# Hash attention and four Fourier-mixing networks on one core: all attention first, masks on TensorE throughout, then the networks in a row

## The chip, the cores and the metric

One Trainium2 chip, one of its cores. The metric is the device time of one execution in microseconds, as the median of several runs. Beside it stands one execution taken by the hardware profiler. TensorE (PE in the profile, its weight loads PEld) multiplies matrices, VectorE (DVE) and ScalarE (ACT) work element by element, GpSimd (POOL) does little here besides issuing transfers, and SyncE (SP) issues most transfers. Every engine runs its own instructions in the order in which they were written for it and waits for the others by semaphores.

## The reference

Batch 4, 8 heads, sequence 768, head size 64; the attention's output, seen as 768 x 512 per batch, goes through a network with a Fourier mixing.

```python
q_bucket = sum((q @ proj > 0) * 2**arange(6)); k_bucket likewise
mask     = q_bucket[..., :, None] == k_bucket[..., None, :]
scores   = where(mask, q @ k.T / sqrt(64), -1e9)
attn     = exp(scores - max); attn = attn / (sum(attn) + 1e-9)
x        = (attn @ v) as (batch, 768, 512)
u        = x + real(fft(fft(x, axis=1), axis=2))
un       = (u - mean(u)) / sqrt(var(u) + 1e-6)
out      = u + relu(un @ w_ch1) @ w_ch2      # 512 -> 2048 -> 512
```

All inputs are float32 except for the weights, which arrive as 64-bit numbers and are narrowed on the chip.

## The kernel before, in words

**Attention.** Two heads make a pair; there are 16 pairs (`n`), four in each batch (`b`). The keys of a pair come in six chunks (`c`) of 128. For one chunk, `scores` (L912) multiplies keys by queries for two halves (`g`) of 384 queries, each half into one of two PSUM buffers `sc`; ACT takes the exponential into a buffer `pk` (L925, of which there are two); `values` (L950) multiplies `pk` into `oo`; a tally (L1044) adds `pk` up on DVE into `acc`, from which `key_sums` (L960) makes the denominators and `scale` the quotient, written to `x`. `prepare` turns queries and keys over and finds their hash bits (L815, L841) for the next pair.

The mask is made in two ways. In pairs 0 to 4 (`LITE`) the hash bits, as plus and minus a large number, are multiplied on TensorE into the same PSUM buffer as the scores (L901), so that a wrong bucket gives an exponential of zero. In pairs 5 to 15 two small matmuls (L855, L865) make bucket numbers, and DVE compares them and multiplies `pk` by the result (L939).

**The network** of a batch, `mix`, has `fold` (DVE sums that use symmetries of the transform and write `z`), two rounds of matmuls `cs` (L1165) and `A`, `B` (L1194) with additions into `x` (L1208), transposes of `x` (`across`, L1220), and `mlp7`. The latter multiplies by a scheme with seven products instead of eight, in an inner half (`inner`: four slices `f` of seven products, L1474, into `h`), an outer half (`outer7`: three groups `j` of seven products, L1353), then a second inner and a second outer half. The left operands of the inner products are sums of quarters of w1, the right ones of the outer products sums of quarters of w2 (the seven names B11 to T4). Network 0 forms them itself: `quarters(f)` makes four sums s1 to s4 in the small buffer `tq` (L1267 to L1270) for the next slice and stores them in DRAM, `weights2` fetches w2, narrows it (`narrow`, L642 to L658) and combines it (L1319 to L1322). Networks 1 to 3 read both back through queues. `tq` also holds temporaries of the outer half, and the spectrum `F` shares its memory with `h`.

**Order.** Attention of batch 0 is written out by hand, with w1 fetched and converted beside it (`weights1`, seven raw buffers). From batch 1 on, `attention(b)` and the network of batch b-1 are generators that a loop advances in turns, so many steps of the network for each chunk; a scheduler with priorities sets the final order, and `behind()` keeps an attention group's matmuls together. Network 3 comes last, alone. PSUM's eight banks are two for `sc`, two for `oo`, two for the rest; only before and after attention may the rest use all of these.

Of the kernel before, what the change touches and what calls it, by code (L numbers as in the profile page):

```python
# [20 lines left out]
P = 128  # L21
# [12 lines left out]
WC = 512  # L34
# [15 lines left out]
def _consts():  # L50
# [23 lines left out]
    pw = np.zeros((P, 2, P))  # L74
    for r in range(P):
        h, bit = divmod(r % 32, NBITS)
        if h < 2:
            pw[r, h] = 2.0**bit


# [13 lines left out]
    for par in range(2):  # L94
# [11 lines left out]
        "pw": np.ascontiguousarray(pw, dtype=np.float32),  # L106
# [379 lines left out]
def _main(  # L486
# [17 lines left out]
    ps_sc = ctx.enter_context(  # L504
        tc.tile_pool(name="ps_sc", bufs=2, space=bass.MemoryType.PSUM)
    )
    ps_o = ctx.enter_context(
        tc.tile_pool(name="ps_o", bufs=2, space=bass.MemoryType.PSUM)
    )
    ps_1 = ctx.enter_context(  # L510
        tc.tile_pool(name="ps_1", bufs=2, space=bass.MemoryType.PSUM)
    )
# [4 lines left out]
    roomy = [True]  # L517
    turn = [0]

    def pt(shape, name):  # L520

        turn[0] += 1
        if roomy[0] and turn[0] % 2:
            if turn[0] % 4 == 1:
                return ps_o.tile(shape, F32, tag="o", name=name)
            return ps_sc.tile(shape, F32, tag="sc", name=name)
        return ps_1.tile(shape, F32, tag="ps", name=name)
# [14 lines left out]
    def load(n, names="qkv", second=nc.sync):  # L542
# [6 lines left out]
        for nm in names:  # L549
            src = {"q": q, "k": k, "v": v}[nm]  # L550
            tag, bufs = ("vn", 2) if nm == "v" else ("qkn", 2)
            tl = wt([P, S], F32, tag, f"{nm}n{n}", bufs)
# [39 lines left out]
    LITE = (0, 1, 2, 3, 4)  # L592
# [6 lines left out]
    own = const.tile([P, 2], F32, tag="own", name="own")  # L599
    nc.sync.dma_start(own, cn["own"].ap())  # L600
    load(0, "v")
    pj = const.tile([P, 32], F32, tag="pj", name="pj")
    nc.gpsimd.memset(pj, 0.0)
    for h in range(2):
        nc.sync.dma_start(pj[h * D : (h + 1) * D, h * NBITS : (h + 1) * NBITS], proj)
    pw = const.tile([P, 2, P], BF16, tag="pw", name="pw")
# [7 lines left out]
    NPK = 2  # L614
    pks = []
    for i in range(NPK):
        pk = const.tile([P, 2, 2, HALF + 1], F32, tag=f"pk{i}", name=f"pk{i}")
        nc.gpsimd.memset(pk[:, :, :, HALF : HALF + 1], EPS)
        pks.append(pk)
# [3 lines left out]
    w2 = const.tile([P, NFC, DM], F32, tag="w2", name="w2")  # L623
# [7 lines left out]
    def narrow(dst, raw, col, low=None):  # L631
# [7 lines left out]
        di = dst.bitcast(I32)  # L639

# [10 lines left out]
        if len(di.shape) == 2:  # L651
            nc.vector.tensor_tensor(di, di, low, op=ALU.add)
        else:
            for i in range(di.shape[1]):
                nc.vector.tensor_tensor(di[:, i], di[:, i], low[:, i], op=ALU.add)
# [38 lines left out]
    class Arrival:  # L694
# [19 lines left out]
        def convert(self, i, low=None):  # L714
            if self.wide:
# [6 lines left out]
                narrow(dst, raw, self.col + i, low)  # L722
            self.fetch(i + self.depth)

    def weights1():
# [6 lines left out]
        ft = wt([P, 12, WC], F32, "F", "fraw", 1)  # L732
        raws = [zt[:, i] for i in range(3)] + [
            ft[:, i : i + 2].rearrange("p i w -> p (i w)") for i in range(0, 8, 2)
        ]
        arrival = Arrival(slices, raws, 0, nc.sync)
        for i in range(arrival.depth):
            arrival.fetch(i)
            if i == 2:
                load(1)  # L740
        yield
        half = None
        for i in range(len(slices)):
            arrival.convert(i, ft[:, 8 + i % 4].bitcast(I32))
            yield
            if half:
                centre(half[0], next(half[1]))
                half = None
            if i % NDC == NDC - 1:


                f = i // NDC * WC
                if f < DFF // 2:
                    half = f, average(f)
                    next(half[1])

# [5 lines left out]
    def norm(n, io, tn):  # L762
        junk = wt([P, S], BF16, "junk", f"sq{io}_{n}", 1)
# [5 lines left out]
    def prepare(n):  # L769

        lite = n in LITE
        ts = {}
        for io, nm in enumerate("qk"):
            tn = nat.pop((nm, n))
            tt = wt([P, S], F32, nm + "t", f"{nm}t{n}")
# [27 lines left out]
        if lite:  # L803

            qk = wt([P, 2, S], BF16, "qb", f"qkb{n}")
            qz = qk[:, 0].rearrange("p (g s) -> p g s", g=2)
            bits = {"q": qz[:, 0], "k": qk[:, 1, 0:HALF]}  # L810
            for io, nm in enumerate("qk"):
                ps = pt([P, HALF], f"bits{nm}{n}")
                for j in range(4):
                    h, g = divmod(j, 2)
                    nc.tensor.matmul(  # L815
                        ps[32 * j : 32 * j + 32, :], pjw[:, h * D : h * D + 32],
                        ts[nm][:, g * HALF : (g + 1) * HALF], start=True, stop=True,
                    )
                nc.vector.tensor_scalar(
                    bits[nm], ps, 0.0, off[:, io : io + 1],  # L820
                    op0=ALU.is_gt, op1=ALU.subtract,
                )
                if io == 0:
                    for g in (1, 0):
                        nc.vector.tensor_scalar(
                            qz[:, g], qz[:, 0], own[:, g : g + 1], None, op0=ALU.mult
                        )
                else:
                    for j in range(4):
                        to, at = (slice(32 * i, 32 * i + 32) for i in (j, j ^ 1))  # L830
                        (evac if n == 0 else nc.vector.tensor_copy)(
# [865 lines left out]
```

## Time and profile before

| | us |
|---|---|
| Median of 3 runs (1073.3 to 1076.49) | 1073.97 |
| Span of the profiled execution, first to last instruction | 1070.7 |
| PE busy | 1036.3 (97%) |
| DVE busy | 779.7 (73%) |
| ACT busy | 489.5 (46%) |
| POOL busy | 64.1 (6%) |

The page gives the profiled execution's span and no other time for it; the median stands 3.3 us above the span, which is taken for what lies around it. A row of the timeline has start, length, engine, line, operation, output and inputs with the shape, and the count; in brackets how long the engine was idle and what ended that. Lengths of pipelined instructions overlap, so costs are best read from start to start. A float32 matmul is two records.

### The profile page before, as it was taken

To read this page: it belongs to the slowest core of one execution; us is meant where nothing else is said; L and a number is where in the kernel's file an instruction comes from. 1 tells how busy PE (TensorE), PEld (TensorE's weight loads), DVE (VectorE), ACT (ScalarE), POOL (GpSimd) and SP (SyncE) were. 2 spreads that over 40 slices of the span, in tenths; PEclk is the share of its full clock that TensorE was granted. 3 is DMA by queue.
4 is the path that set the end of the run, shared out by engine and by line. 5 is a ranking of instruction groups with operands and counts; after the bars stand their busy time and mean duration, and the time that the engine had idled before them with its cause. 6 is when DMAs were issued, how large, how long until landed. Compare 5 with 4: busy or idle time off the path is not lost.

```text
span 1070.7 us, 14177 instructions
## 1 busy us (share of the span) xinstructions
PE 1036.3 (97%) x4983; PEld 635.7 (59%) x4983; DVE 779.7 (73%) x1326; ACT 489.5 (46%) x993; POOL 64.1 (6%) x138
## 2 busy tenths in 40 slices
PE   8999899999999999999999999999999999999997
PEld 4333364457644676546665675555675579668576
DVE  4889969996799967877758877767857874644353
ACT  7888564761386323454236315354325512440420
POOL 2000000011000020100000020010000012200000
PEclk9999999999999999999999999999999999999999
DMA  8754551480154462123062242322042205222301
GB/s 192 217 141 86 113 139 41 135 234 1 35 150 158 125 202 37 44 67 80 12 201 74 66 121 90 59 64 60 15 130 81 65 25 172 65 74 92 125 20 43
DMA packets 172769, 103.15 MB, mean 96 GB/s; under 512 B 126481, under 2 KB 159889, under 8 KB 172689
## 3 DMA queue, kind: packets, MB, share of 16 engines
q1 hardware_dynamic: 166672, 88.25, 30.4%
q0 software_dynamic: 4448, 13.50, 4.2%
q8 instruction: 42, 0.69, 0.3%
q10 hardware_dynamic: 1568, 0.39, 0.2%
q14 instruction: 39, 0.31, 0.1%
HBM read 81.14 MB, written 20.97 MB: 95 GB/s over the span
## 4 chain that ended last, share of the span: by engine, by line
PE 76%; DVE 14%; ACT 4%; issue 2%; DMA 2%; SPq 1%; DVEq 0%; ACTq 0%; POOL 0%; POOLq 0%
PE o L1353 25%; PE h_p L1474 23%; PE oo L950 10%; PE sc L912 9%; PE cs L1165 3%; DVE pk L939 2%; PE A L1194 2%; DVE acc L1044 2%; ACT pk L925 2%; PE B L1194 1%; PE sum L960 1%; SPq L576 1%; DVE x L1208 1%; PE bits L841 1%; DMA qn<-in_q_dram 1%
## 5 line engine op out<-in xcount | busy, mean ns | idle before, releaser
L1353 PE MATMUL o<-w,h 128*128 128x256 f32 x1152 | 258.6, 381 | 0.9 <-DVE w L1365 0.5
L1353 PEld LDWEIGHTS o<-w,h 128*128 128x128 f32 x1152 | 216.7, 190 | 41.6 <-issue 6.4
L925 ACT ACTIVATE pk<-sc 128x768 f32<-128x768 f32 x192 | 147.4, 808 | 78.7 <-PE oo L950 35.8
L1474 PE MATMUL h_p<-x,w 128*128 128x384 f32 x448 | 164.5, 494 | 2.4 <-ACT w L1541 1.7
L939 DVE SCALAR_TENSOR_TENSOR pk<-qb,kb,pk 128x768 f32<-128x768 bf16 x132 | 128.7, 1011 | 39.7 <-ACT pk L925 39.6
L912 PE MATMUL sc<-qt,kt 64*128 64x384 f32 x768 | 153.6, 503 | 1.7 <-ACT pk L925 1.4
L950 PE MATMUL oo<-pk,vn 128*64 128x385 f32 (+1 forms) x768 | 146.2, 495 | 1.5 <-DVE pk L939 1.3
L1474 PEld LDWEIGHTS h_p<-x,w 128*128 128x128 f32 x448 | 81.9, 190 | 68.4 <-issue 9.3
L1474 PE MATMUL h_p<-w 128*128 128x384 f32 x288 | 105.9, 489 | 0.0
L1044 DVE TENSOR_TENSOR acc<-acc,pk 128x1536 f32<-128x1536 f32 (+1 forms) x64 | 98.5, 1549 | 5.4 <-ACT pk L925 5.2
L950 PEld LDWEIGHTS oo<-pk,vn 128*64 128x64 f32 x768 | 50.5, 136 | 86.5 <-issue 74.2
L912 PEld LDWEIGHTS sc<-qt,kt 64*128 64x128 f32 x768 | 66.2, 186 | 55.4 <-issue 19.3
L1474 PEld LDWEIGHTS h_p<-w 128*128 128x128 f32 x288 | 53.7, 190 | 38.8 <-issue 1.6
L1365 DVE SCALAR_TENSOR_TENSOR w<-o,rs,w 128x256 f32<-128x256 f32 x56 | 26.6, 479 | 41.6 <-PE o L1353 41.6
L1383 ACT COPY tq<-o 128x256 f32<-128x256 f32 x24 | 8.9, 372 | 104.5 <-PE o L1353 104.5
L1488 ACT ACTIVATE h<-h 128x384 f32<-128x384 f32 x72 | 37.4, 524 | 28.5 <-DVE h L1530 13.7
L1353 PE MATMUL o<-w 128*128 128x256 f32 x176 | 42.2, 383 | 0.3 <-DVE w L1365 0.2
L1103 POOL DMA_DIRECT2D out_dram<-w x30 | 16.4, 548 | 405.3 <-issue 321.4
L1525 DVE TENSOR_TENSOR h<-h 128x384 f32<-128x384 f32 x32 | 17.7, 555 | 28.9 <-ACT h L1524 28.8
L1353 PEld LDWEIGHTS o<-w 128*128 128x128 f32 x176 | 32.9, 190 | 7.6 <-DVE w L1365 1.2
L1399 DVE TENSOR_TENSOR tq<-tq,o 128x256 f32<-128x256 f32 x24 | 10.0, 417 | 36.4 <-PE o L1353 36.4
L1372 ACT COPY tq<-o 128x256 f32<-128x256 f32 x24 | 8.8, 369 | 60.3 <-PE o L1353 60.2
(175 smaller groups left out, 1316.1 us busy)
## 6 DMA issues: line engine op xcount, KB each, us to landing
w<-ad SPq DMA_DIRECT2D x168, 128.0 KB, 2.1
w<-bd SPq DMA_DIRECT2D x42, 512.0 KB, 4.5
zraw<-in_moe_w_ch_dram POOLq DMA_DIRECT2D x16, 512.0 KB, 3.8
bd<-w SPq DMA_DIRECT2D x14, 512.0 KB, 3.6
vn<-in_v_dram SPq DMA_DIRECT2D x32, 192.0 KB, 3.4
qn<-in_q_dram SPq DMA_DIRECT2D x116, 48.0 KB, 2.5
kn<-in_k_dram SPq DMA_DIRECT2D x58, 96.0 KB, 2.9
zraw<-in_moe_w_ch_dram SPq DMA_DIRECT2D x8, 512.0 KB, 7.1
```

The source lines that it names most:

```text
L912: last[0] = nc.tensor.matmul(ps[:, h, 0:HALF], kt[rows, ks], qt[rows, qs], start=kb is not None or early, stop=not early,)
L925: done_by[ET.Activation] = nc.scalar.activation(pk[:, g, :, 0:HALF], ps[:, :, 0:HALF], AF.Exp, scale=SCALE)
L939: done_by[ET.DVE] = nc.vector.scalar_tensor_tensor(w, qb[:, h].rearrange("p (g s) -> p g s", g=2), kb[:, h, c : c + 1], w, op0=ALU.is_equa ...
L950: oo = nc.tensor.matmul(oos[g][h * D : (h + 1) * D, 0:w], nat["v", n][:, (2 * c + h) * D : (2 * c + h + 1) * D], pk[:, g, h, 0:w], start=( ...
L1044: done_by[ET.DVE] = nc.vector.tensor_tensor(acc[:, g], (first if c == 1 else acc)[:, g], new[:, g], op=ALU.add,)
L1165: nc.tensor.matmul(ps[:, pc + 2 * lo : pc + 2 * hi - 1 : 2], z[:, cp, pc, par, t * P : (t + 1) * P], ch[:, cp, pc, lo:hi], start=(cp == 0) ...
L1194: nc.tensor.matmul(ps[:, cols], F[:, par, k, t, j * P : (j + 1) * P], sq[:, t, k, cols], start=(t == 0), stop=(t == 1),)
L1353: nc.tensor.matmul(ps, a[:, r], right7[i][:, r], start=start and r == 0, stop=r == HF // 2 - 1, skip_group_check=not start,)
L1365: nc.vector.scalar_tensor_tensor(t[:, cols], src, r, t[:, cols], op0=ALU.mult, op1=ALU.add)
L1474: nc.tensor.matmul(ps, left[:, k], right[i][:, k], start=start and k == 0, stop=k == 1, skip_group_check=not start,)
L1488: done_by[ET.Activation] = nc.scalar.activation(h, h, AF.Relu)
L1525: done_by[ET.DVE] = nc.vector.tensor_tensor(c22, c21, c22, op=ALU.add)
```

## The change

- `attention` runs over all 16 pairs in one loop, written out by hand: scores of a chunk, then `values` and tally of the chunk before, with the next pair's `prepare`, a step of `weights1` (three a pair from pair 1 on) and, in the last pair, the fold of batch 0. Key and query loads run two pairs ahead.
- The mask is on TensorE in every pair; `LITE`, the bucket numbers, the mask on DVE, `behind` and the key sums in several parts are gone. All five tallies are DVE additions of 1536 columns.
- There are four `pk` buffers. `x` has one buffer for each batch.
- The attention's memory (`att`) and PSUM pools are closed after the last pair; w2, `tq`, `F`/`h` and a pool of eight PSUM banks are opened in it. The four networks run one after the other. The fold of batch b+1 is written into the second outer half of network b.

```diff
-    LITE = (0, 1, 2, 3, 4)
-    NPK = 2
+    NPK = 4
...
+            first = None
+            for c in range(NT):
+                pk = scores(n, c)
+                first = pk if c == 0 else first
+                done = pending.pop(0) if pending else None
+                if c == 1:
+                    next(ends[0][0], None) if ends else None
+                if done:
+                    m, d, dpk, doos, dfirst, dacc = done
+                    values(m, d, dpk, doos)
+                    tally(d, dpk, dfirst, dacc)
+                    if d == NT - 1:
+                        ends.append([scale(m, doos, dacc)])
+                        next(ends[-1][0])
+                if ends and c in (2, 3):
+                    next(ends[0][0], None)
...
+                if c < NT - 1 if n else c:
+                    next(ahead, None)
+                if n and c in (0, 4, 5):
+                    next(other, None)
+                if c > 1:
+                    next(folds, None)
+                pending.append((n, c, pk, oos, first, acc))
...
+    own.close()
+    late = ctx.enter_context(tc.tile_pool(name="late", bufs=1, reuse_waits="tile"))
+    ps_b = ctx.enter_context(
+        tc.tile_pool(name="ps_b", bufs=8, space=PSUM, reuse_waits="tile")
+    )
...
-            yield from outer7(b, half, hall, ut, rs, ss)
+            ahead = fold(b + 1) if half and b < B - 1 else iter(())
+            for _ in outer7(b, half, hall, ut, rs, ss):
+                next(ahead, None)
+                yield
+            for _ in ahead:
+                pass
...
     for b in range(B):
...
-            for i, _ in enumerate(attention(b), 1):
...
-                while done * steps < (MIX - LEFT) * (i - wait):
-                    next(other)
-                    done += 1
...
         other = mix(b)
         if b == 0:
...
-            other = after(NT, other, islice(arrival2, HF + 2))
+            other = after(NT - 2, other, islice(arrival2, HF + 2))
+        for _ in other:
+            pass
```

On TensorE, the end of a pair in batch 2 before (`oo` of a pair among products `o` of network 1's outer half; two heads share the array when their matmuls stand next to each other):

```order
L1353 MATMUL o_1_0_0_4123<-w_124,h_3092 128x256 x4
L950 MATMUL oo_0_3861<-pk_117,vn_3489 64x385
L1353 MATMUL o_1_0_4_4143<-w_124 128x256 x4
L1353 MATMUL o_1_0_6_4151<-w_124,h_3092 128x256 x4
L1353 MATMUL o_1_0_4_4143<-w_124,h_3092 128x256 x4
L1353 MATMUL o_1_0_5_4164<-w_124,h_3092 128x256 x4
L950 MATMUL oo_0_3861<-pk_117,vn_3489 64x385
L950 MATMUL oo_1_3862<-pk_117,vn_3489 64x384 x2
```

and a chunk of a late pair after the change (L834 masks, L844 scores, L860 values, L878 key sums):

```order
L844 MATMUL sc_0_1_2580<-qt_2395,kt_2421 128x384 x2
L834 LDWEIGHTS qkb_2452
L834 MATMUL sc_1_1_2586<-qkb_2452 128x384
L834 LDWEIGHTS qkb_2452
L834 MATMUL sc_1_1_2586<-qkb_2452 128x384
L844 MATMUL sc_1_1_2586<-qt_2395,kt_2421 128x384 x2
L878 MATMUL sum_2592<-acc_2373,ones 32x384 x4
L860 MATMUL oo_0_2548<-pk_119,vn_2368 64x385 x2
L860 MATMUL oo_1_2549<-pk_119,vn_2368 64x384 x2
```

The network's matmuls are gone from between the two heads' matmuls, and masks have come in.

On DVE, the fold of batch 0 before (L1125 to L1143, between preparations of the next pair and, further on, of pair 5; L1044 is the tally):

```order
L1044 TENSOR_TENSOR acc_845<-acc_845,pk_119 128x768 x2
L1125 TENSOR_TENSOR ef_0_0_953<-x_209 128x768
L1130 TENSOR_TENSOR ef_0_0_953<-ef_0_0_953 128x384 x2
L1139 TENSOR_TENSOR z_952<-ef_0_0_953 128x2x95
L1139 TENSOR_TENSOR z_952<-ef_0_0_953 128x2x96
L1139 TENSOR_TENSOR z_952<-ef_0_0_953 128x2x95
L1139 TENSOR_TENSOR z_952<-ef_0_0_953 128x2x96
L1143 COPY z_952<-ef_0_0_953 128x2x2
L819 TENSOR_SCALAR qkb_964<-bitsq_965,off 128x384
```

and after the change, in pair 15, the last (L906 tally, L940 to L958 fold, L885 the first step after the last key sums):

```order
L906 TENSOR_TENSOR acc_2877<-acc_2877,pk_119 128x1536
L940 TENSOR_TENSOR ef_1_1_3028<-x_193 128x768
L945 TENSOR_TENSOR ef_1_1_3028<-ef_1_1_3028 128x384 x2
L954 TENSOR_TENSOR z_2947<-ef_1_1_3028 128x2x95
L954 TENSOR_TENSOR z_2947<-ef_1_1_3028 128x2x96
L954 TENSOR_TENSOR z_2947<-ef_1_1_3028 128x2x95
L954 TENSOR_TENSOR z_2947<-ef_1_1_3028 128x2x96
L958 COPY z_2947<-ef_1_1_3028 128x2x2
L906 TENSOR_TENSOR acc_2877<-acc_2877,pk_121 128x1536
L940 TENSOR_TENSOR ef_0_0_3934<-x_887 128x768
L885 STREAM_TRANSPOSE rt_3051<-sum_3046 128x384
```

All four pieces of the fold, of which this is the fourth, stand between two tallies each, ahead of the last tally.

On DVE in network 0, at the turn from slice 1 to slice 2 (after the change; L1400 to L1424 add into `h`, the last of a slice being L1424; L620, L624 and L637 narrow w2, L1148 to L1151 are s1 to s4 of the next slice):

```order
L1412 TENSOR_TENSOR h_3234<-h_3234,w_3074 128x384
L1416 TENSOR_TENSOR h_3234<-h_3234 128x384
L1148 TENSOR_TENSOR tq<-w_125 128x256
L1150 TENSOR_TENSOR tq<-w_125 128x256
L1424 TENSOR_TENSOR h_3234<-h_3234,w_3074 128x384
L1149 TENSOR_TENSOR tq<-tq,w_125 128x256
L620 TENSOR_SCALAR w_3074<-zraw_3080 128x2x256
L1151 TENSOR_TENSOR tq<-w_125,tq 128x256
L624 SCALAR_TENSOR_TENSOR w_3074<-zraw_3080,w_3074 128x2x256
L637 ISA w_3074<-zraw_3080,w_3074 128x512 x2
```

Before, the same place (L1518 to L1542 add into `h`, L1267 to L1270 are s1 to s4, L642 to L655 narrow) held attention's masks and tallies between them:

```order
L1542 TENSOR_TENSOR h_1465<-h_1465,w_124 128x384
L655 ISA w_124<-zraw_1083,w_124 128x512 x2
L1269 TENSOR_TENSOR tq<-w_123 128x256
L1270 TENSOR_TENSOR tq<-w_123,tq 128x256
L939 SCALAR_TENSOR_TENSOR pk_117<-qb_1257,kb_1258,pk_117 128x2x384
L1518 TENSOR_TENSOR h_1465<-h_1465 128x384
L939 SCALAR_TENSOR_TENSOR pk_117<-qb_1257,kb_1258,pk_117 128x2x384
L1044 TENSOR_TENSOR acc_1386<-acc_1386,pk_117 128x1536
```

What is left on DVE there is the network's own work and the conversion of w2.

467 lines of the change are left out of this document (154 added, 313 removed).

## The prediction, made before the changed kernel was run

> **What bounds the kernel now.** I read the page's busy shares and chain first, then the busy time stage by stage, then TensorE's timeline of one stretch where attention runs alone, and last the timelines of VectorE (DVE) and ScalarE (ACT) where they are fullest.
>
> ```profile
> PE 1036.3 (97%) x4983; PEld 635.7 (59%) x4983; DVE 779.7 (73%) x1326; ACT 489.5 (46%) x993; POOL 64.1 (6%) x138
> ...
> PE 76%; DVE 14%; ACT 4%; issue 2%; DMA 2%; SPq 1%; DVEq 0%; ACTq 0%; POOL 0%; POOLq 0%
> ```
>
> TensorE is busy for 97% of the span and carries 76% of the chain. A reordering can therefore win only idle time and badly packed matmuls; otherwise it pays for every matmul that it adds. So I price both kernels in TensorE time without gaps, and then add the gaps.
>
> The last network runs with no attention beside it. These rows give its five stages (mixing; inner half, outer half, inner, outer) and their sum:
>
> ```profile
> 897.40:916.80 19.40, 18.99 (x125) 18.29 (x125) 11.75 (x24) 4.67 (x14) 1.74 (x4) 1.00 0.24 83
> 916.80:954.40 37.60, 37.60 (x126) 22.56 (x125) 16.82 (x34) 20.23 (x43) 5.39 (x12) 1.00 0.31 92
> 954.40:990.70 36.30, 36.30 (x170) 31.95 (x169) 18.61 (x37) 4.65 (x12) 0.00 (x0) 1.00 0.24 78
> 990.70:1026.80 36.10, 36.10 (x114) 21.26 (x113) 12.06 (x23) 17.13 (x37) 0.00 (x0) 1.00 0.28 89
> 1026.80:1063.20 36.40, 36.40 (x169) 31.72 (x167) 18.67 (x38) 4.65 (x12) 0.00 (x0) 1.00 0.13 34
> sum 165.80, PE 165.39 PEld 125.78 DVE 77.91 ACT 51.33 POOL 7.13; mean PE 33.08 PEld 25.16 DVE 15.58 ACT 10.27 POOL 1.43
> ```
>
> Columns: window, length, then PE, PEld, DVE, ACT, POOL busy, clock, DMA. A network alone is 165.8 us with TensorE idle for 0.4, and DVE has half of that free. The stage before it was the previous network's outer half, so the seam between two networks has no gap either.
>
> Attention alone, in the first batch, masks on TensorE; then a chunk of a later pair whose masks are on DVE; last the final matmuls:
>
> ```profile
> 9.29 0.92 PE L912 MATMUL sc<-qt,kt 64*128 64x384 f32 x4
> ...
> 86.31 0.85 PE L960 MATMUL sum<-pk,ones 128*32 128x384 f32 x8
> 87.10 0.34 PE L901 MATMUL sc<-qkb 64*128 64x384 bf16 x2
> ...
> 91.69 0.34 PE L901 MATMUL sc<-qkb 64*128 64x384 bf16 x2
> 91.87 0.81 PE L912 MATMUL sc<-qt,kt 64*128 64x384 f32 x4
> ...
> 93.41 1.51 PE L950 MATMUL oo<-pk,vn 128*64 128x385 f32 x8
> 94.86 0.34 PE L901 MATMUL sc<-qkb 64*128 64x384 bf16 x2
> ...
> 101.18 0.85 PE L815 MATMUL bitsq<-qt,pjw 128*32 128x384 f32 x8
> 101.97 0.34 PE L901 MATMUL sc<-qkb 64*128 64x384 bf16 x2
> ...
> 150.14 1.56 PE L912 MATMUL sc<-qt,kt 64*128 64x384 f32 x8
> 151.63 1.51 PE L950 MATMUL oo<-pk,vn 128*64 128x385 f32 x8
> 153.07 0.92 PE L1194 MATMUL A<-sq,F 128*128 128x193 f32 x4
> ...
> 1057.87 5.34 PE L1353 MATMUL o<-w,h 128*128 128x256 f32 x24
> ```
>
> Columns: start, length. From start to start a chunk with masks takes 94.86 - 91.69 = 3.17 us, one without 153.07 - 150.14 = 2.93; a set of bits 0.79 (101.18 to 101.97), a set of key sums 0.79. Scores begin at 9.29. The last matmul ends at 1063.2, and the span 7.5 us later, in stores that the change keeps.
>
> **The change, part by part.** Its fixed cost, from these groups:
>
> ```profile
> L939 DVE SCALAR_TENSOR_TENSOR pk<-qb,kb,pk 128x768 f32<-128x768 bf16 x132 | 128.7, 1011 | 39.7 <-ACT pk L925 39.6
> L667 PE MATMUL ws<-w,ones 128*32 128x512 f32 x32 | 4.2, 601 | 3.1 <-DVE qkb L819 2.4 <-DVE rt L982 0.7
> L675 PE MATMUL wm<-part,mean 128*128 128x512 f32 x8 | 4.2, 631 | 0.3 <-ACT part L672 0.3
> L855 PE MATMUL qb<-bt,pw 32*128 32x384 bf16 x44 | 5.5, 326 | 0.0
> L865 PE MATMUL kb<-pw,bt 32*128 32x2 bf16 x66 | 2.6, 164 | 0.0
> ```
>
> All masks on TensorE: 66 chunks of 11 pairs get 3.17 - 2.93 = 0.24 us each, 15.8, and 11 second sets of bits at 0.79, 8.7. Gone are the bucket numbers, 5.5 + 2.6 = 8.1, the second and third sets of key sums in the first four pairs, some 6, and DVE's 128.7 us of masks. TensorE pays about 10 us more; DVE is relieved, but it was not the bound.
>
> Order: nothing stands between attention's matmuls any more, nor between the network's. Without gaps, a pair is 6 x 3.17 + 2 x 0.79 + 0.79 = 21.4 us (six chunks, two sets of bits, one of sums). So: start 9.3, 16 pairs 342, weight averages 4.2 + 4.2 = 8.4, four networks at 165.8 = 663.2, end 7.5. That is 1030.4. The span before was 1070.7, so all gaps together may reach 40 before the gain is gone. The same count for the kernel before gives 1020, so it loses 50 to gaps and to packing broken by interleaving; the new order removes those, and brings gaps of its own:
>
> Attention alone. Is TensorE kept fed? DVE adds all five tallies of a pair now (it had three or four), and converts w1 beside them. The nearest row is a pair that did that under more load:
>
> ```profile
> 67.60:90.90 23.30, 22.80 (x164) 8.90 (x160) 21.84 (x37) 22.86 (x45) 0.00 (x0) 1.00 0.57 99
> ```
>
> DVE busy 21.84 and ACT 22.86 of 23.30, and TensorE waited 0.5. After the change a pair converts 1.2 slices of w1 instead of six, and there are four pk buffers for two. I take 0.2 a pair, 3 in all (ends 0 and 0.5 x 16 = 8; a centring of four subtractions could add to it), and 1 for the first pair. Key and query loads run two pairs ahead instead of one; their queue, SP, loses the wait behind seven w1 fetches, so I cost loads at nothing.
>
> End of attention. The four pieces of the fold of batch 0 now stand between the tallies of the last pair:
>
> ```profile
> 82.45 0.69 ACT L650 ACTIVATE fraw<-fraw 128x512 int32<-128x512 uint32 x1
> ...
> 84.65 1.50 ACT L925 ACTIVATE pk<-sc 128x768 f32<-128x768 f32 x2
> 86.04 0.69 ACT L650 ACTIVATE fraw<-zraw 128x512 int32<-128x512 uint32 x1
> ...
> 107.95 0.95 DVE L1125 TENSOR_TENSOR ef<-x 128x768 f32<-128x768 f32 x1
> ...
> 111.14 0.61 DVE L819 TENSOR_SCALAR qkb<-bitsk,off 128x384 bf16<-128x384 f32 x1
> ...
> 125.66 1.75 DVE L1044 TENSOR_TENSOR acc<-pk,pk 128x1536 f32<-128x1536 f32 x1
> ```
>
> A piece is 111.14 - 107.95 = 3.2 us, a tally 1.75, an ACT conversion 84.65 - 82.45 = 2.2. In pair 15 the second pk is ready 3.17 + 0.8 + 1.5, about 5.8 us in. From there DVE has five tallies, 8.75, four pieces, 12.8, and about 2.8 of the previous pair's scaling: done at 30.1. TensorE is through with its own chunks at 6 x 3.17 + 0.79 + 1.44, 21.3, and its next instruction, the last key sums, needs the last tally. Idle: 9 us (ends 5 and 12).
>
> That gap has a second price, at the first matmuls after it. At the start of this kernel stands:
>
> ```profile
> L582 PE MATMUL busy<-mean 128*128 128x128 f32 x18 | 4.2, 430 | 1.0 <-POOL warm L585 1.0
> ```
>
> 18 passes of 128 columns took 4.2 us, 234 ns each; in the outer half above a pass of 256 columns took 36.30/170 = 214 ns. So the first 4 us of a rested array ran at half rate. No gap in the trace after that shows whether 9 us rest the array, so my sum holds nothing for it; the range does, up to 2. The Trainium skill (TensorE: Matmul & The Clock Gate, "What's actually happening") says that an idle window of about 3.4 us halves the clock until it has been busy as long. By that rule the sum would be an estimated 2 us more, 1066; the start of this trace agrees with it, no later row here can. Both sums lie inside my own case below.
>
> Network 0. It converts w2 and forms the quarter matrices (tq) for slice f + 1 while it computes; attention used to fill TensorE meanwhile.
>
> ```profile
> L1514 ACT COPY h<-h_p 128x384 f32<-128x384 f32 x32 | 15.3, 478 | 18.6 <-PE h_p L1474 18.6
> ...
> 211.14 0.68 DVE L646 SCALAR_TENSOR_TENSOR w<-zraw,w 128x512 int32<-128x512 int32 x1
> 211.74 0.41 DVE L1321 TENSOR_TENSOR w<-w 128x256 f32<-128x256 f32 x1
> 212.08 0.41 DVE L655 CUSTOM_DVE_ANT_0 w<-zraw,w 128x512 uint16<-128x512 uint16 x1
> ...
> 213.08 0.55 DVE L1530 TENSOR_TENSOR h<-h,w 128x384 f32<-128x384 f32 x1
> 213.55 0.55 DVE L1534 TENSOR_TENSOR h<-h 128x384 f32<-128x384 f32 x1
> ```
>
> Back to back, DVE needs 0.34 us for an operation of 256 columns, 0.47 for an add of 384, 0.60 for the wide one; a conversion 0.34 + 0.60 + 2 x 0.34 = 1.6. Each half adds eight conversions, 12.9, and 16 combinations and 16 quarters, 10.9: with the stages above DVE comes to 11.75 + 16.82 + 23.8 = 52.4 of 57.0 in the first half and 12.06 + 23.8, 35.9 of 36.1, in the second. It just fits, but it is in order. A slice is 36.1/4 = 9.0 us of seven products, 1.29 each. The second product of a slice needs s2 (L1149 after), which stands behind the last add of the slice before: copy 0.48, add 0.47, one to two quarters, three hand-overs, some 2 us, against one product, 1.29, of cover. So 0.7 at least, more where a conversion stands between: I take 1 for each of 8 slices, 8. To it: 3 before the first slice (two conversions stand among the adds of the mixing), 2 at the turn of the halves (the outer half still writes tq), 3 in the second outer half (T4 comes late, and three fold pieces of batch 1, 9.6 us, join DVE's 18.67/3 = 6.2 in a third of 12.1). 16 in all; ends 5 (only the floor) and 30 (ACT's conversion of 2.2 before each copy).
>
> Networks 1 and 2: the fold of the next batch lies in a DVE that is half free; 1 each, for adds of the mixing that wait behind it (ends 0 and 4).
>
> Sum: 1030.4 + 1 + 3 + 9 + 16 + 2 = 1061.4. The median of the runs, 1073.97, lies 3.3 above the profiled span; with it the time is 1064.7, I say 1064.
>
> **Rivals.** A, slower: network 0 is bound by DVE and ACT. For it speak 35.9 of 36.1 and an ACT with 17.13 plus eight conversions of 2.2, 34.7 of 36.1; against it, that the pair above ran at 94% and 98% with a loss of 0.5. At 30 and with the other upper ends halfway the span is 1082, time 1085; it turns the sign from 25 on. B, faster: the waits for s2 and the fold's tail are half hidden, 1030.4 + 1 + 0 + 5 + 8 + 0, time 1048. For it speaks that the scheduler had freedom there; against, that the order below the seam puts the tallies behind the fold. C, no change: attention's tallies and ACT's uneven visits (a conversion, a norm and the copies of a chunk against 3.17 - 1.4 of free ACT) cost 0.8 a pair, 13 instead of 3: time 1075.
>
> **The numbers.** My forecast 0.50, A 0.20, B 0.15, C 0.15. A measurement tells 0.3%, 3.2 us, from no change. Of my own case (1056 to 1075) 0.42 lies below 1070.8, with B 0.57; half of C, some of mine and of A make 0.18; slower 0.25. The range, 1046 to 1086, reaches over B and C and most of A.
>
> **What would show it.** Right: chunks of 3.17 in a row with waits under 0.5 us a pair; one idle stretch of TensorE of 7 to 11 us before the last key sums, released by DVE acc; in network 0 waits of about a microsecond each slice, released by DVE tq; networks 1 to 3 each within 3 us of 165.8. Wrong: waits of scores for ACT in every chunk; network 0 beyond 192; a gap between two networks, or matmuls at half rate for long after the gap.

## The result, and the profile after

The changed kernel takes 1062.39 us (median of 4 runs, 1062.13 to 1063.04), the kernel before 1075.23 in the same comparison: ratio 0.9886, 95% interval 0.9871 to 0.9902. The span of the profiled execution went from 1070.7 to 1060.3. 1064 had been predicted; it will be seen that this sum came out partly because errors in it cancel.

The page, first group, clock row and chain:

```profile
PE 1025.1 (97%) x5161; PEld 646.3 (61%) x5161; DVE 681.2 (64%) x1215; ACT 500.3 (47%) x1009; POOL 65.2 (6%) x139
...
PEclk9899999999999989999999999999999999999998
...
PE 86%; DVE 7%; ACT 4%; DMA 1%; issue 1%; SPq 0%; POOL 0%; DVEq 0%; ACTq 0%; POOLq 0%
```

TensorE has 178 more matmul records and yet 11 us less busy time: they stand behind one another now. DVE has lost 98 us of busy time. The chain is TensorE's for 86%, 76 before. The clock row, the granted clock of TensorE in 40 equal slices of the span, has 8s in slices 2, 15 and 40; before it was all 9s.

Attention, the masks of two chunks of pair 15 in a row (start, length, engine, line):

```profile
354.86 0.34 PE L834 MATMUL sc<-qkb 64*128 64x384 bf16 x2
...
358.03 0.34 PE L834 MATMUL sc<-qkb 64*128 64x384 bf16 x2
```

One chunk takes 3.17 us (354.86 to 358.03). What TensorE waited for over the whole program (total, times, longest):

```profile
PE sum L878 <- DVE acc L906: 8.8, 1, 8.8
PE sc L834 <- ACT pk L850: 8.2, 7, 5.8
PE h_p L1356 <- DVE tq L1149: 2.7, 3, 1.4
PE h_p L1356 <- ACT h L1396: 1.8, 4, 0.6
```

Two stalls stand out, one foreseen and one not. The foreseen one, before the last key sums, on TensorE and on DVE:

```profile
366.08 2.81 PE L860 MATMUL oo<-pk,vn 128*64 128x385 f32 x16
377.73 1.51 PE L878 MATMUL sum<-acc,ones 128*32 128x384 f32 x8 [8.85 <-DVE acc L906]
379.17 8.78 PE L1033 MATMUL cs<-ch,z 128*128 128x129 f32 x48
...
555.80 7.19 PE L1033 MATMUL cs<-ch,z 128*128 128x129 f32 x48
```

```profile
366.20 1.75 DVE L906 TENSOR_TENSOR acc<-acc,pk 128x1536 f32<-128x1536 f32 x1
367.87 0.95 DVE L940 TENSOR_TENSOR ef<-x 128x768 f32<-128x768 f32 x1
...
371.06 1.75 DVE L906 TENSOR_TENSOR acc<-acc,pk 128x1536 f32<-128x1536 f32 x1
...
375.92 1.75 DVE L906 TENSOR_TENSOR acc<-acc,pk 128x1536 f32<-128x1536 f32 x1
```

TensorE stands 8.85 us while DVE does a piece of the fold (L940 to L958) between each two tallies. Behind the gap the key sums take 1.51 us in place of 0.85, and the first product of the mixing (`cs`) takes 8.78 in place of the 7.19 of network 1, the last line.

The other stands in pair 1, where 5.84 of the 8.2 us of waits for `pk` fall; TensorE, ACT and SyncE:

```profile
36.54 1.51 PE L860 MATMUL oo<-pk,vn 128*64 128x385 f32 x8
43.90 0.51 PE L834 MATMUL sc<-qkb 64*128 64x384 bf16 x2 [5.84 <-ACT pk L850]
44.17 1.51 PE L844 MATMUL sc<-qt,kt 64*128 64x384 f32 x4
...
48.90 0.85 PE L786 MATMUL bitsq<-qt,pjw 128*32 128x384 f32 x8
```

```profile
40.83 0.68 ACT L628 ACTIVATE low<-zraw 128x512 int32<-128x512 uint32 x1 [6.08 <-DMA zraw<-in_moe_w_ch_dram]
...
43.05 1.49 ACT L850 ACTIVATE pk<-sc 128x768 f32<-128x768 f32 x2
```

```profile
25.12 2.05 SPq L552 DMA_DIRECT2D kn<-in_k_dram  x4
34.15 0.97 SPq L546 DMA_DIRECT2D vn<-in_v_dram  x2
35.16 8.34 SPq L689 DMA_DIRECT2D zraw<-in_moe_w_ch_dram  x4
```

Read from the last of these views: SyncE has issued the keys of pair 3 by 27.2 and then stands until 34.15, since the values of pair 2 (L546) go into the buffer of pair 0's values, which TensorE used until then. The first fetch of w1 (L689) is behind them in the queue. The first conversion (L628) waits for it on ACT, and the exponential of pair 1's second chunk (L850) stands behind the conversion.

The networks (window, length, then PE, PEld, DVE, ACT, POOL busy, clock):

```profile
379.17:555.80 176.63, 170.02 (x700) 126.05 (x697) 134.59 (x312) 81.39 (x186) 22.23 (x41) 0.99 0.41 142
555.80:721.23 165.43, 165.11 (x697) 125.98 (x696) 88.03 (x182) 51.29 (x118) 15.19 (x29) 1.00 0.32 100
721.23:886.99 165.76, 165.44 (x700) 126.15 (x699) 86.38 (x180) 51.18 (x118) 14.81 (x30) 1.00 0.32 99
```

Network 0 takes 11 us more than the others; between networks there is no wait.

### The profile page after: what moved, and what is told of

Read it like the earlier page. It is cut to its first block, busy times and chain, and to the rows that moved or that the text cites. A ratio compares the mean times of both kernels' runs of the same rounds, so it can differ in the third digit from the quotient of the medians.

```text
span 1060.3 us, 14379 instructions
## 1 busy us (share of the span) xinstructions
PE 1025.1 (97%) x5161; PEld 646.3 (61%) x5161; DVE 681.2 (64%) x1215; ACT 500.3 (47%) x1009; POOL 65.2 (6%) x139
## 4 chain that ended last, share of the span: by engine, by line
PE 86%; DVE 7%; ACT 4%; DMA 1%; issue 1%; SPq 0%; POOL 0%; DVEq 0%; ACTq 0%; POOLq 0%
PE o L1235 26%; PE h_p L1356 24%; PE oo L860 11%; PE sc L844 10%; PE sc L834 3%; PE cs L1033 3%; PE B L1062 1%; PE A L1062 1%; ACT pk L850 1%; DMA zraw<-in_moe_w_ch_dram 1%; PE bitsq L786 1%; PE bitsk L786 1%; PE sum L878 1%; PE un L1088 1%; DVE acc L906 1%
## 5 line engine op out<-in xcount | busy, mean ns | idle before, releaser
L1235 PE MATMUL o<-w,h 128*128 128x256 f32 x1152 | 254.1, 379 | 0.3 <-DVE h L1263 0.3
L850 ACT ACTIVATE pk<-sc 128x768 f32<-128x768 f32 x192 | 153.0, 810 | 79.1 <-PE sc L844 79.1
L1356 PE MATMUL h_p<-x,w 128*128 128x384 f32 x448 | 160.4, 488 | 2.0 <-ACT h L1396 1.8
L844 PE MATMUL sc<-qt,kt 64*128 64x384 f32 x768 | 156.7, 486 | 0.0
L860 PE MATMUL oo<-pk,vn 128*64 128x385 f32 (+1 forms) x768 | 145.3, 499 | 0.0
L906 DVE TENSOR_TENSOR acc<-acc,pk 128x1536 f32<-128x1536 f32 x64 | 112.0, 1750 | 23.8 <-ACT pk L850 23.8
L860 PEld LDWEIGHTS oo<-pk,vn 128*64 128x64 f32 x768 | 46.7, 136 | 88.5 <-issue 78.0
L844 PEld LDWEIGHTS sc<-qt,kt 64*128 64x128 f32 x768 | 69.3, 190 | 20.9 <-issue 20.7
L834 PE MATMUL sc<-qkb 64*128 64x384 bf16 x384 | 64.3, 329 | 8.7 <-ACT pk L850 8.2
L834 PEld LDWEIGHTS <-qkb 64*128 64x128 bf16 x384 | 19.8, 93 | 82.1 <-issue 61.9
L906 DVE TENSOR_TENSOR acc<-pk,pk 128x1536 f32<-128x1536 f32 x16 | 28.0, 1751 | 27.4 <-ACT pk L850 27.4
L1407 DVE TENSOR_TENSOR h<-h 128x384 f32<-128x384 f32 x32 | 17.8, 556 | 42.2 <-ACT h L1406 42.2
L1400 DVE TENSOR_TENSOR h<-h 128x384 f32<-128x384 f32 x32 | 17.8, 556 | 30.4 <-ACT h L1399 30.3
```

The lines of the kernel that those rows point to most:

```text
L834: nc.tensor.matmul(ps[:, h, 0:HALF], qk[rows, 1, at : at + P], qk[rows, 0, g * HALF : (g + 1) * HALF], start=start, stop=not start,)
L844: nc.tensor.matmul(ps[:, h, 0:HALF], kt[rows, ks], qt[rows, qs], start=early, stop=not early,)
L850: nc.scalar.activation(pk[:, g, :, 0:HALF], ps[:, :, 0:HALF], AF.Exp, scale=SCALE)
L860: nc.tensor.matmul(oos[g][h * D : (h + 1) * D, 0:w], nat["v", n][:, (2 * c + h) * D : (2 * c + h + 1) * D], pk[:, g, h, 0:w], start=(c == ...
L906: nc.vector.tensor_tensor(acc, (first[:, :, :, 0:HALF] if c == 1 else acc), new, op=ALU.add)
L1235: nc.tensor.matmul(ps, a[:, r], right7[i][:, r], start=start and r == 0, stop=r == HF // 2 - 1, skip_group_check=not start,)
```

## The experiments

Executions differ in when their first scores come (the section on the hardware says from what in part), so beside the ratio the table has, from each profile, the first scores, the attention from there to the first product of the mixing, and network 0 from there to network 1's (us):

| kernel | ratio to before (95%) | first scores | attention | network 0 |
|---|---|---|---|---|
| the change | 0.9886 (0.9871 to 0.9902) | 10.17 | 369.0 | 176.6 |
| w1 fetched in pair 0 | 0.9825 (0.9812 to 0.9839) | 11.48 | 361.0 | 177.1 |
| fold earlier | 0.9867 (0.9852 to 0.9882) | 12.03 | 363.5 | 177.5 |
| both | 0.9793 (0.9780 to 0.9806) | 9.99 | 357.3 | 176.1 |
| matmuls in the gap | 0.9910 (0.9894 to 0.9925) | 10.27 | 368.0 | 177.1 |
| masks left out from pair 5 | 0.9777 (0.9762 to 0.9792) | 9.62 | 355.4 | 176.4 |
| old order, all masks on TensorE | 1.0110 (1.0095 to 1.0126) | 8.89 | | |
| quarters summed once | 0.9872 (0.9857 to 0.9887) | 11.58 | 368.5 | 173.2 |
| both, second buffer for quarters | 0.9721 (0.9708 to 0.9734) | 10.28 | 352.8 | 172.6 |
| all PSUM pools at the start | 0.9894 (0.9879 to 0.9909) | 11.29 | 368.7 | 177.0 |
| two `pk` buffers | 1.0088 (1.0072 to 1.0103) | 10.33 | 392.2 | 177.7 |
| all four moves | 0.9712 (0.9699 to 0.9726) | 9.97 | 352.9 | 172.9 |
| and pair 1's loads on SyncE | 0.9713 (0.9699 to 0.9726) | 8.96 | 352.8 | 173.2 |

**The fetch of w1 in pair 0.**

```diff
-            if n == 1:
+            if n == 0:
                 next(other)
```

> The changed kernel, with the first fetch of the first weights called in pair 0, behind the values of pair 1, in place of pair 1, behind the values of pair 2; nothing else is moved. Theory: in the changed kernel the fetch left SyncE only at 35.2 us, because the values of pair 2 wait there for the buffer of pair 0's values; its data came at 40.8, VectorE and ScalarE stood at their first conversion until then, the exponentials stood behind it on ScalarE, and TensorE had a gap of 5.8 us, after which its matmuls took about twice as long for some 3 us. With the fetch at about 21 us the gap goes and so do the long matmuls: 6 to 7.5 us less than the changed kernel, ratio to the kernel before 0.982 (the changed kernel had 0.9886). Rival one: the fetch takes its share of the DMA queues from the loads of pair 1 and pair 2 at the start, and what is gained comes back as waits for those loads: 0 to 3 us less. Rival two: the slack is taken up by network 0 or the end of attention, no gain.

SyncE, and TensorE at the place of the stall:

```profile
20.81 1.49 SPq L689 DMA_DIRECT2D zraw<-in_moe_w_ch_dram  x3
```

```profile
39.04 0.34 PE L834 MATMUL sc<-qkb 64*128 64x384 bf16 x2
...
42.20 0.85 PE L786 MATMUL bitsq<-qt,pjw 128*32 128x384 f32 x8
```

The gap is gone, and from the scores to the bits it is 3.16 us (39.04 to 42.20) where it was 5.00 (43.90 to 48.90): the stall's price was 5.84 and another 1.84 of slow matmuls. The attention is 8.0 us shorter and the ratio 0.0061 lower, 6.5 us. No wait of TensorE for the loads of pairs 1 and 2 has come in its place. The first theory is shown.

**The fold earlier.**

```diff
-            folds = fold(0) if n == NPAIR * B - 1 else iter(())
+            if n == NPAIR * B - 2:
+                folds = fold(0)
...
-                if c > 1:
+                if (n, c) in ((14, 3), (15, 0), (15, 1), (15, 3)):
                     next(folds, None)
```

> The changed kernel, with the four pieces of the fold of batch 0 (3.1 us of VectorE each) put into pair 14 (one) and the first, second and fourth visit of pair 15, in place of the last four visits of pair 15. Theory: the gap of 8.85 us before the last key sums is VectorE's two last tallies standing behind two pieces of the fold; with the pieces done by then, the last key sums wait for two tallies at most (1.75 us each, some 3 us behind the last exponential), and TensorE's first product behind the gap is no longer slowed: a gap of 1 to 3 us, and 7 to 9 us less than the changed kernel, ratio to the kernel before 0.980. Rival: the pieces in pairs 14 and 15 hold up the scale of the pair before or the bits of pair 15 on VectorE, and the gaps stand inside the pairs: less than 4 us gained.

TensorE behind the last values:

```profile
374.78 0.85 PE L878 MATMUL sum<-acc,ones 128*32 128x384 f32 x8 [4.22 <-DVE acc L906]
375.56 8.96 PE L1034 MATMUL cs<-ch,z 128*128 128x129 f32 x48
```

The gap shrank by 4.6, not by 6 or more, and the attention by 5.5; the medians are only 2.0 us apart, and the intervals overlap. The forecast of 7 to 9 us failed, since tallies still end late and the product behind the gap is still slow (8.96). What is late shows on DVE, in the kernel with both moves, where the gap is the same 4.22:

**Both.** The two edits together.

> Both of these moves in the changed kernel. Theory: they are two places with no common part, so the gains add: 13 to 16.5 us less than the changed kernel, span about 1045, ratio 0.974. Rival (a fixed total elsewhere, such as VectorE's or the DMAs' work, sets the end): the sum is smaller than the parts by over 3 us.

```profile
358.82 1.76 DVE L906 TENSOR_TENSOR acc<-acc,pk 128x1536 f32<-128x1536 f32 x1
360.49 0.95 DVE L940 TENSOR_TENSOR ef<-x 128x768 f32<-128x768 f32 x1
...
361.95 1.75 DVE L906 TENSOR_TENSOR acc<-acc,pk 128x1536 f32<-128x1536 f32 x1
363.62 0.55 DVE L945 TENSOR_TENSOR ef<-ef 128x384 f32<-128x384 f32 x1
364.09 1.75 DVE L906 TENSOR_TENSOR acc<-acc,pk 128x1536 f32<-128x1536 f32 x1
```

There is still a piece of fold between the tallies: batch 1's first, which belongs to network 0 and which the scheduler puts forward into DVE's row (in the changed kernel it stands right behind the last tally). And one of the four pieces ended only as these tallies began. The two moves add: attention and network 0 together are 12.2 us shorter than in the changed kernel, against 7.6 and 4.6 for each alone (the ratios say 10.0, 6.5 and 2.0; the fold's kernel had its first scores 1.9 us later in its profile). So the sum of the parts holds, but not the 13 to 16.5 us, for the fold gave less than was expected of it.

**Matmuls in the gap.**

```diff
+        ps = pt([P, P], "warm2")
+        for _ in range(36):
+            nc.tensor.matmul(ps, mean, mean, start=True, stop=True)
         tally(d, dpk, dfirst, dacc)
```

> The changed kernel, with 36 matmuls of 128x128 on constants (about 0.21 us each, 7.6 us together; their result is not used) in TensorE's row between the last values and the last key sums, where it waits 8.85 us for VectorE. The gap's length is set by VectorE and stays. Theory of a clock that falls when TensorE idles: the last key sums take 0.81 in place of 1.51 us and the first product of batch 0's mixing 7.2 in place of 8.8, so 2.0 to 2.4 us less than the changed kernel. Rival: these were long for another reason (the first use of the new memory, a wait for the tables of cosines), and stay so: the time doesn't change, or it is longer by what the 36 matmuls run past the gap.

```profile
377.46 0.85 PE L878 MATMUL sum<-acc,ones 128*32 128x384 f32 x8 [0.62 <-DVE acc L906]
378.24 1.16 PE L1036 MATMUL cs<-ch,z 128*128 128x129 f32 x8
379.88 6.40 PE L1036 MATMUL cs<-ch,z 128*128 128x256 f32 x40 [0.48 <-DVE rt L885]
```

With TensorE busy in the gap the key sums take 0.85 again and the product 8 of its matmuls in 1.16 and 40 in 6.40. The granted clock is 1.00 from 368.53 to 386.10, where it was 0.50 at the key sums of the changed kernel. So the slow matmuls came from the idleness, as the first theory says. But its 2.0 to 2.4 us did not come: the time is not better (0.991; the intervals overlap). The product now waits 0.48 for DVE's reading of the key sums; TensorE is 1.67 us ahead at the end of the mixing (396.55 against 398.22) and 0.46 at the end of network 0 (555.34 against 555.80), since the waits for ACT's `h` there have become 2.8 us from 1.8. The clock's price is real on TensorE, and here most of it is taken up by what stands next.

**Masks left out from pair 5.**

```diff
-            if not early:
+            if n < 5 and not early:
                 masks(True)
```

> The changed kernel without the mask matmuls of pairs 5 to 15 (66 chunks; the bits are still made, every weight of these pairs counts as a match, so the sums are other ones); all else is kept. Theory: in the new order the attention is TensorE's, chunk by chunk, so each mask costs what its matmuls take on TensorE, 0.24 us a chunk: 66 x 0.24 = 15.8 us less than the changed kernel, ratio to the kernel before 0.974, and a chunk takes 2.93 us. Rival: ScalarE (12 to 14 of 21 us a pair) or VectorE (16 of 21) sets the pace as soon as TensorE has less, and waits of the scores for the exponentials take its place: less than 8 us gained.

From the key sums of pair 4 to those of pair 14, without masks and, below, with them, each from its own kernel:

```profile
130.41:338.50 208.09, 206.08 (x1233) 75.88 (x1231) 176.68 (x223) 160.94 (x297) 0.00 (x0) 1.00 0.45 94
```

```profile
131.83:352.62 220.79, 219.67 (x1472) 84.88 (x1470) 176.32 (x223) 166.16 (x297) 0.00 (x0) 1.00 0.42 89
```

60 chunks are 12.7 us shorter, 0.21 each of the 0.24 predicted; idle time grew from 1.1 to 2.0. In the last pair nothing is gained, for DVE sets its end (the gap there is 9.82). By the ratios the whole gain is 11.7 us, not 15.8. So in the new order the masks are paid on TensorE almost in full, and neither ScalarE nor VectorE sets the pace, but for the last pair.

**The masks moved alone**, in the kernel before:

```diff
-    LITE = (0, 1, 2, 3, 4)
+    LITE = tuple(range(16))
```

> The kernel before, with the masks of all 16 pairs on TensorE in place of the first five; its order, its networks between the pairs and its two weight buffers are kept: the part of the change that moves the masks, alone. Theory: TensorE gets 66 x 0.24 = 15.8 us of masks and 11 x 0.79 = 8.7 of bits and loses 8.1 of bucket numbers, and VectorE's 128.7 us of masks were beside it: 8 to 17 us slower than the kernel before, ratio 1.007 to 1.016, so the new order must bring some 20 to 28. Rival: VectorE's masks stand in the chain between the exponential and the values, and without them the 50 us that TensorE idles in the kernel before shrink by more than it gains in work: ratio 0.97 to 0.995.

```profile
PE 1047.1 (97%) x5225; PEld 641.0 (59%) x5225; DVE 680.0 (63%) x1249; ACT 482.0 (45%) x982; POOL 60.8 (6%) x138
```

11.2 us slower in the medians, with 10.8 more of TensorE's busy time (1036.3 before); by the items of the prediction it would be 15.8 + 8.7 - 8.1 = 16.4. The span without TensorE's busy time is 34.4 us before and 35.2 here, so VectorE's 100 us less have shortened no waits on balance; what is missing to 16.4 is missing in the busy time itself. The rival falls. The other parts of the change, order and buffers, are thus worth 0.0224, 24 us. In the profiles they are 22.0 us, all of it in TensorE's busy time (1047.1 against 1025.1): in the changed kernel, too, the span without it is 35.2. So the new order did not remove idle time on balance; it put long gaps (5.84 and 8.85) in the place of many short ones (none above 2.0 in the old order), and what it won is shorter work, 6.7 us of it the 64 records of key sums from `pk` that are gone.

**Quarters summed once.**

```diff
+        if f == 0:
             nc.vector.tensor_tensor(s1, a21, a22, op=ALU.add)
...
```

> The changed kernel, with VectorE's four sums of the first weights' quarters in network 0 made for slice 0 only (the other seven slices multiply by slice 0's sums; 28 operations of 0.42 us, 11.8 us of VectorE, are gone; their stores stay). Theory, as predicted: TensorE's waits in network 0 for these sums are their being late, so these three waits (2.7 us) go, the rest of network 0's loss (11 us over network 1, of which 1.7 is the slow first product) stays: 2 to 4 us less than the changed kernel, ratio 0.985 to 0.987. Rival one: VectorE as a whole sets network 0's pace, and with 11.8 us less of it the waits for ScalarE's and VectorE's other results go too: 6 us or more less, ratio below 0.983. Rival two: the waits move to the next late result: no change.

Network 0 is 3.4 us shorter in the profile; the waits for `tq` (2.7) are gone, those for ACT's `h` (L1397) have become 2.7 from 1.8. By the ratios the gain is 1.5 us, and the intervals overlap. The 6 us or more that VectorE as the bound would have given did not come.

**Both, and a second buffer.** The fold's pieces move on to visits 3, 3, 0 and 1 of pairs 13, 14, 15 and 15, and batch 1's fold is held in its place:

```diff
+    tr = late.tile([P, 4, HD], F32, tag="tr", name="tr")
...
-        st = tq[:, 0:4].rearrange("p i (k m) -> p i k m", m=P)
+        st = (tr if f % 2 else tq)[:, 0:4].rearrange("p i (k m) -> p i k m", m=P)
...
-                next(ahead, None)
+                with in_turn():
+                    next(ahead, None)
```

> The changed kernel with the fetch in pair 0, the fold's pieces in visits 3, 3, 0 and 1 of pairs 13, 14, 15 and 15, the fold of batch 1 held behind the work around its place in network 0 (the scheduler had put its first piece between the last two tallies of pair 15), and a second buffer for the sums of quarters in network 0. Theory: the gap before the last key sums goes from 4.2 us (both moves) to under 1.5, TensorE's clock doesn't fall there (2 us), and the waits for the sums of quarters (2.7 us) go: 5 to 8 us less than both moves, 1043 to 1046, ratio 0.972. Rival: VectorE is 16 of 21 us busy in pairs 13 and 14 as it is, and the pieces there make the scores wait; and network 0 waits for other results in the place of the sums: 0 to 3 us less than both moves.

```profile
359.47 2.81 PE L860 MATMUL oo<-pk,vn 128*64 128x385 f32 x16
362.31 0.85 PE L878 MATMUL sum<-acc,ones 128*32 128x384 f32 x8
363.09 7.29 PE L1034 MATMUL cs<-ch,z 128*128 128x129 f32 x48
```

No gap and no slow matmul is left at the end of attention, and network 0 is at 172.6. With 1043.31 us the kernel lies in the range of the first theory. Three things were changed at once: that the second buffer acts in network 0 and the rest in the attention shows by place, but how much of the 4.22 us went with the earlier pieces and how much with the fold held in its place is not separated. Holding the fold costs networks 1 and 2 half a microsecond each (166.0 and 166.3).

**Two `pk` buffers.** `NPK = 2` in the changed kernel. The first addition of a pair then reads the third chunk's weights where it should read the first's, and so waits for their exponentials too; the work is the same.

> The changed kernel with two buffers of weights in place of four: one of the parts of the change undone. Theory: two buffers make the exponential of a chunk wait for the values and the tally of the chunk two before it; VectorE's tallies come up to 5 us behind the exponentials in the changed kernel, so the scores wait for ScalarE and ScalarE for VectorE in many chunks: 10 to 40 us slower than the changed kernel, ratio 0.998 to 1.026. Rival: VectorE has 5 us to spare in a pair and only orders itself otherwise: within 4 us of the changed kernel, ratio 0.985 to 0.9925.

21.7 us slower than the changed kernel (0.0202), nearly all in the attention. Here waits like those of rival C of the prediction are to be seen, in total, times, and longest:

```profile
PE sc L834 <- ACT pk L850: 20.2, 13, 5.9
PE sum L878 <- DVE acc L906: 6.4, 1, 6.4
```

Within the attention TensorE is idle for 31.8 us (17.6 in the changed kernel) and busy for 360.5 (351.4). The longer work is in part slow matmuls behind these waits, of which the last section shows one.

**The start.** The kernel before took PSUM from all three pools until attention began.

```diff
+        banks[0] = roomy
         for _ in prepare(0):
             pass
+        banks[0] = small
```

> The changed kernel, with the accumulators of the preparation of pair 0 taken in turn from all three pools of PSUM, as the kernel before took them, in place of the one pool of two buffers; the rest is kept. Theory: the first scores come at 9.3 us (8.9 in the old order with all masks) where pair 0 has the three pools, and at 9.6 to 12.0 in the changed kernel and its variants, because the second transposes wait there for the copies of the first ones out of the same two buffers (0.9 us on ScalarE's copy of q in the changed kernel, 1.7 to 1.8 us in three variants); with room the first scores come by 9.3 and the time is 1 to 2.5 us less than the changed kernel, ratio to the kernel before 0.9865 to 0.988. Rival: the start follows the arrival of the first loads, which differs from run to run, and the first scores stay between 9.6 and 12.

The transposes of `k` start at 7.61, in the changed kernel at 7.57: the theory falls. The wait has only another name, the load of `k`:

```profile
7.61 1.03 PE L761 MATMUL trk<-ident,kn 128*128 128x128 f32 x6 [1.65 <-DMA kn<-in_k_dram]
```

That the first scores came only at 11.29 is the two sets of bits behind this wait, which took 1.51 each in place of 0.85.

The same with the other moves:

> The kernel with the early fetch, the earlier fold, the second buffer for sums of quarters, and the three pools for the preparation of pair 0 as well. Theory: the parts lie in different places and add: 1 to 2.5 us less than without the pools at the start, 1041 to 1042.5 us, ratio 0.970 to 0.9715. Rival: no gain at the start, 0.972.

The ratio, 0.9712, lies in the theory's range, but its interval takes in that of the kernel without these pools (0.9721), and the first scores come only 0.3 us earlier: a gain is not shown.

Why `k` of pair 0 is late shows in the transfers: in the changed kernel GpSimd issues six loads of pair 1 from 1.85 us on, which it issued from 8.40 on before. So the last kernel issues them on SyncE, behind pair 0's own:

```diff
-            (nc.gpsimd if n == 1 and r else nc.sync).dma_start(d[r], s[r])
+            nc.sync.dma_start(d[r], s[r])
...
```

> The kernel with all four moves, and the loads of pair 1 issued by SyncE alone, behind the values of pair 0, in place of six of the twelve by GpSimd (which issues them from 1.85 us on in the changed kernel and from 8.40 us on in the kernel before, where it waits). Theory: the transposes of pair 0's k wait for its load (1.65 us in the kernel with room at the start, 0.48 in the kernel before), since it shares the DMA engines with those six loads; without them k lands by 6.9 us in place of 7.5, the first scores come at 9.0 to 9.3 us in place of 9.97, and the time is 0.7 to 1.5 us less than with all four moves, ratio 0.970 to 0.9708. Rival: pair 1's q and k now come some 2 us later, their transposes stand in VectorE's row in front of pair 0's tallies, and the first pair gets longer by that: no gain or up to 2 us slower.

```profile
6.76 0.85 PE L761 MATMUL trk<-ident,kn 128*128 128x128 f32 x6 [0.70 <-DMA kn<-in_k_dram]
```

`k` is there 0.8 us earlier and the first scores come at 8.96 in place of 9.97. This 1 us is seen in the profile alone; the ratios, 0.9712 and 0.9713, can't tell it. The best of these kernels take 1042 to 1043 us, 2.8 to 2.9% less than the kernel before.

## Why the prediction was right, and where it was not

- **What bounds the kernel: right.** Work added to TensorE is paid and work taken from VectorE is not: 16.4 us for the masks by its items, 11.2 measured with them alone in the old order, and 0.21 of 0.24 us for each chunk in the new one.
- **Attention kept fed: right, but for "I cost loads at nothing".** Chunks are 3.17; the waits for `pk` outside the one stall are 8.2 - 5.8 = 2.4 us in 16 pairs, 0.15 each against 0.2. With two buffers they are 20.2 - 5.9 = 14.3, near the 13 of rival C. The step that failed is the one on the loads: the queue lost the wait behind seven fetches of w1, but the first of those that are left was put behind a load that waits for a buffer. That cost 5.84 us and 1.84 of slow matmuls, as moving it showed. The same step failed at the start: 9.3 in the sum, 10.17 measured, from loads of pair 1 that no longer wait.
- **End of attention: right.** 9 predicted, 8.85 measured, released by `acc`. The reason holds in the trace of the changed kernel, where DVE goes from tally to piece without a pause, and the gap went when the fold was out of the way.
- **The clock behind the gap** was left out of the sum: 0.66 + 1.59 = 2.3 us of longer matmuls. The 2 that the range held for it was the right size. That with the gap filled so little of it would be won in the end was not foreseen.
- **Network 0: the mechanism right, the size not.** 16 predicted over a network alone; measured 176.6 - 165.8 = 10.8, of which 1.6 is the slow product, so 9.2. The term that was mis-sized most is the 8 for the wait for s2: it came in 3 slices of 8, 2.7 us in all. In the others TensorE did not wait for them. The 3 for the second outer half were too much as well: it shows one wait, of 0.3. With 9.2 the network lies nearer to the 8 of rival B than to the forecast's 16. Without these sums, or with a second buffer, 3.4 and 4.1 us went (the latter with the slow product's 1.5).
- **Networks 1 and 2:** 165.4 and 165.8, so nothing where 2 stood.
- **The sum:** the stall (7.7), the clock (2.3) and the start (0.9) were missing, 10.9; network 0 (6.8) and the two later networks (2) held 8.8 too much, and attention without the stall and the slow key sums some 3. The span was predicted at 1061.4 and is 1060.3. That a sum with errors of 7 in both directions is right to 0.1% is luck; what bounds the kernel, the chunk and the gap are what was understood.

## What to carry to other kernels

Where an engine issues transfers in order, a transfer is as late as the slowest wait ahead of it (here SyncE stood from 27.2 to 34.15 us): after a reordering, read the issuing queue for a load that waits for a buffer, and for one that no longer does. Work that fills slack must be done before the last dependent step, not spread over it; and look at where the scheduler has put it, and what it has put in its place (here a piece of the next stage's fold). Before booking the slow matmuls behind a gap as a gain, ask what stands next.

## What was not expected of the hardware

TensorE's matmuls were slow behind each long gap, and there the granted clock was half: 5.84 us idle, then 1.51 in place of 0.81 for a set of scores; 8.85 idle, then 1.51 in place of 0.85 for the key sums. The first of these, from the changed kernel (columns as for the networks, the clock third from the end):

```profile
43.90:47.20 3.30, 3.30 (x12) 1.49 (x11) 2.56 (x4) 2.28 (x4) 0.00 (x0) 0.50 0.69 182
```

The Trainium skill (TensorE: Matmul & The Clock Gate, "What's actually happening") says that an idle window of about 3.4 us halves the clock until TensorE has been busy as long; these two gaps agree with it.

Shorter gaps of these runs do not fit it. With two `pk` buffers the clock fell to 0.50 behind four of five waits of 2.05 to 2.07 us; here is one, from TensorE's timeline, with the clock behind it:

```profile
133.09 0.34 PE L834 MATMUL sc<-qkb 64*128 64x384 bf16 x2 [2.05 <-ACT pk L850]
```

```profile
134.00:135.20 1.20, 1.20 (x8) 0.69 (x5) 1.20 (x1) 0.47 (x1) 0.00 (x0) 0.50 0.82 293
```

Behind the fifth, at 229.22, it stayed at 1.00. At the start it fell to 0.50 behind waits of 1.65 to 1.78 us in four kernels (w1 fetched in pair 0, the fold earlier, quarters summed once, and all PSUM pools at the start), and these are the four whose first scores came last, at 11.29 to 12.03. Behind 1.50, with all four moves, and behind 1.36, the longest wait inside network 0, it stayed at 1.00. So in this case a gap of half that window could halve the clock, and need not.

Two gaps of the same 4.22 us differed too: with the fold earlier, the key sums behind it took 0.85 and the product 8.96; with both moves 1.51 and 8.04:

```profile
365.89 1.51 PE L878 MATMUL sum<-acc,ones 128*32 128x384 f32 x8 [4.22 <-DVE acc L906]
367.33 8.04 PE L1034 MATMUL cs<-ch,z 128*128 128x129 f32 x48
```

With the fold earlier the clock was full through the whole gap and fell only when TensorE was at work again:

```profile
370.50:374.78 4.28, 0.06 (x3) 0.01 (x1) 4.22 (x4) 0.70 (x2) 0.00 (x0) 1.00 0.00 0
375.56:379.00 3.44, 3.44 (x17) 3.06 (x14) 2.31 (x5) 1.44 (x6) 0.00 (x0) 0.54 0.02 5
```

The loss is about the same (1.77 and 0.66 + 0.85 = 1.51 us), but the slow stretch did not begin at once in the first. What sets its beginning no run here shows.
